# Retention and a gated feed-forward layer on one core: operand sums gated on VectorE's, loads moved five groups ahead of preparation, weight sums and evacuations moved, the last tile's products cut in pieces

## The chip, the cores and the metric

The kernel runs on one core of one Trainium2 chip. The metric is the device time of one execution in microseconds (us). A core has five engines with instruction queues of their own: TensorE (PE, with its weight loads PEld), VectorE (DVE), ScalarE (ACT), GpSimd (POOL) and SyncE (SP, which here only issues DMAs). SBUF is the working memory, PSUM the banks into which TensorE writes.

## The reference

```python
def _attn_ref(q, k, v):                      # (8, 8, 576, 64) each
    scores = scale * np.matmul(q, k.transpose(0, 1, 3, 2))
    gamma = 1.0 - 2.0 ** (-5.0 - np.arange(H))
    rel = pos[:, None] - pos[None, :]
    Dmat = np.where(rel >= 0, gamma[:, None, None] ** rel[None, :, :], 0.0)
    return np.matmul(scores * Dmat[None], v)
def _moe_ref(x, w_in, w_out):                # x: 4608 x 512, w_in: 512 x 2048, w_out: 2048 x 512
    h = x @ w_in
    return (h * np.cos(h)) @ w_out
# out = moe(attention output, the heads side by side in 512 columns)
```

Inputs and output are float32; inside, the matmul operands are bf16.

## The kernel before, in words

The 4608 tokens are 36 **groups** of 128, and ten **tiles**: one of 512 tokens (tile 0), two of 256 (tiles 1 and 2) and seven of 512 (tiles 3 to 9; `S7 = 3` is the first of these). The manual schedule keeps every engine's instructions in the order in which the Python code issues them; between engines the framework puts semaphores wherever a tile is written and read.

**Per group.** `load` issues the DMAs of fq, fk and fv (256 KB each, 128 tokens by 8 heads by 64) on SP's queue into a pool of five buffers each. `prep` runs on GpSimd: it multiplies fq and fk with the decay factors into `qks` (lines 137 and 138) and casts fv to `vb` (144). `transposes` is, from group 6 on, a DMA transpose `qks` to `qkT` on SP (153); it can't be issued before GpSimd has finished that group's `qks`. `scores` is 8 matmuls and a VectorE multiplication with the causal mask to `ret` (180, 189). `states` forms the running state in PSUM bank "b", VectorE accumulates it to `s` (260, 262) and ScalarE copies it to `sb` (253). `attn_out` puts state and scores together (280, 293), and ScalarE casts the result to `xT` (305). `unit7(g)` does this for two groups: states of g+1 and g+2, attention output of g and g+1, then scores of g+2 and g+3 (banks "a" and "b", so the second scores need bank "b" free of the states).

**Per tile.** `mm1` computes the hidden layer in eight blocks of 1024 columns: 8 matmuls, ScalarE's cosine (328), VectorE's gating multiplication to `gT` (329). In tiles 3 to 9 the second matrix product is done in the seven products of a Strassen scheme (`mm2_seven`), in the order 3, 4, 5, 2, 1, 7, 6, each 16 matmuls of 256 columns (`product`, line 430). Products 3 and 4 read `gT`; the other five read **operand sums** `gs` of quarters of `gT` (`g_sum`, 395). `sums_after` issues these in two halves, after blocks 3 and 7 of `mm1`: sum 5 on VectorE, sums 2, 1, 7 and 6 on GpSimd, each 128 x 1024. The weight sums `ws` for products 1, 6 and 7 are made once, by VectorE (373); in the kernel before between the gating multiplications of tile 2. The results are put together in four output tiles `ot` by ScalarE copies and VectorE additions (459 to 478) and stored.

**What sets the order.** Behind each store `mm2_seven` calls `feed`, which issues the preparation, transposes and loads of later groups. Each call works on the queue entries of two engines: SP gets the transpose (which waits for GpSimd) and then the next load behind it; GpSimd gets `prep`. So GpSimd's queue holds, for each of tiles 4 to 6, eight operand sums and then four preparations (tile 7 has two preparations, tiles 8 and 9 have only the sums). `at` says ahead of which product a `unit7` stands.

Of the kernel before, what the change touches and what calls it, by code (L numbers as in the profile page):

```python
# [17 lines left out]
def kernel(  # L18
# [16 lines left out]
    nc = tc.nc  # L35
# [20 lines left out]
    N_PE_T = 6  # L56

    consts = ctx.enter_context(tc.tile_pool(name="consts", bufs=1))
    first = ctx.enter_context(tc.tile_pool(name="first", bufs=1))
    ld = ctx.enter_context(tc.tile_pool(name="ld", bufs=5))  # L60
# [319 lines left out]
    def g_sum(n, x, e0, e1):  # L380
# [14 lines left out]
        (nc.vector if x == 5 or (n, x) == (S7, 1) else nc.gpsimd).tensor_tensor(  # L395
            out=tiles["gs", n, x][:, e0:e1], in0=i0, in1=i1, op=op_
        )

# [14 lines left out]

    def product(n, x):

        gT = tiles["g", n]
        if x in (3, 4, 1, 7):
            ps = psum.tile([P, 2, N2], F32, tag={3: "n", 4: "st", 1: "n", 7: "st"}[x], name="o")
            tiles["o", x] = ps
        else:  # L420
            ps = tiles["o", {5: 3, 2: 4, 6: 1}[x]]
# [6 lines left out]
        for e in range(E2):  # L428
            for j in range(2):
                nc.tensor.matmul(  # L430
                    ps[:, j],
                    lhsT=lhs[:, e, j * P : (j + 1) * P],
                    rhs=rhs[:, e, :],
                    start=(x in (3, 4, 1, 7) and e == j == 0),
                    stop=(e == E2 - 1 and j == 1),
                    skip_group_check=True,
                )

    def mm2_seven(n, at):

        s0 = starts[n] // P

# [10 lines left out]
        for x in (3, 4, 5, 2, 1, 7, 6):  # L453
            for u in at.get(x, []):
                u()
            product(n, x)
            if x == 3:
                u22 = new("a")
                nc.scalar.copy(u22, tiles["o", 3])
            elif x == 4:  # L460
                nc.vector.tensor_tensor(out=u22, in0=tiles["o", 4], in1=u22, op=ALU.add)
            elif x == 5:
                c12, u11 = new("c"), new("b")
                nc.scalar.copy(c12, tiles["o", 3])
                nc.vector.tensor_tensor(out=u11, in0=u22, in1=tiles["o", 3], op=ALU.subtract)
                store(c12, 0, 1, s0)
            elif x == 2:
                c21 = new("d")
                nc.scalar.copy(c21, tiles["o", 4])
                nc.vector.tensor_tensor(out=u22, in0=u22, in1=tiles["o", 4], op=ALU.subtract)  # L470
                store(c21, 1, 0, s0 + 1)
            elif x == 1:
                nc.vector.tensor_tensor(out=u11, in0=tiles["o", 1], in1=u11, op=ALU.add)
            elif x == 7:
                nc.vector.tensor_tensor(out=u11, in0=tiles["o", 7], in1=u11, op=ALU.add)
                store(u11, 0, 0, s0 + 2)
            elif x == 6:
                nc.vector.tensor_tensor(out=u22, in0=tiles["o", 1], in1=u22, op=ALU.add)
                store(u22, 1, 1, s0 + 3)

    loaded = prepared = transposed = 4

    def feed(s):
# [155 lines left out]
    def unit7(g, more=True):  # L639

        copy = states([g + 1, g + 2], "b")()
        attn_out([g, g + 1], "m", nc.scalar.copy)
        if more:
            scores2(g + 2)
        copy(nc.scalar.copy)

    late = []
    for n, w in enumerate(widths):
# [14 lines left out]
        for i, (et, c0, cw) in enumerate(blocks):  # L663
# [16 lines left out]
        if n == 0:  # L680
            todo = [
                (45, lambda: transposes(4, "ab")),
# [62 lines left out]
```

## Time and profile before

| | |
|---|---|
| median of 14 runs | 323.14 us (321.73 to 325.9) |
| the profiled execution | 322.88 us; span from first to last instruction 321.1 us, 1.78 us lie around it |
| mean granted TensorE clock | 0.992 |
| busy: PE / DVE / ACT / POOL | 293.2 / 209.7 / 139.3 / 218.7 us |
| PE waits for GpSimd's operand sums | 6.7 us at matmuls (7 waits), 9.0 us at weight loads (8 waits), overlapping each other |
| GpSimd's first step of a preparation waits for the fq DMA | 56.2 us, 21 waits, longest 17.4 us |

The busy times are sums over stages with different limits, so the prediction reads them tile by tile. Rows of the timeline begin with the start and the duration in us; in brackets stands the idle time of that engine just before, and what ended it. "x8" after a shape counts instructions merged in one row. SPq is SP's issuing of DMAs.

### The profile page before, as it was taken

What the parts mean: (1) busy time and instruction counts of PE and PEld (TensorE: products, weight loads), DVE (VectorE), ACT (ScalarE), POOL (GpSimd) and SP (SyncE); (2) the same over time, 40 slices, a digit from 0 to 9 for tenths busy, and PEclk for the clock granted to TensorE, in tenths of its full rate; (3) what the DMA queues carried; (4) which work ended last, traced back from release to release, by engine and by line L of the source; (5) the groups of instructions that cost most, each with busy time, mean ns of one, the idle gap of its engine ahead of it and who ended that gap; (6) DMA issues with size and microseconds to landing.
All of it is one profiled execution on the core that took longest, in us unless ns stands there. A gap on an engine that the chain in (4) does not pass through costs nothing.

```text
span 321.1 us, 6585 instructions
## 1 busy us (share of the span) xinstructions
PE 293.2 (91%) x2724; PEld 199.3 (62%) x2745; DVE 209.7 (65%) x242; ACT 139.3 (43%) x176; POOL 218.7 (68%) x179
## 2 busy tenths in 40 slices
PE   8899999996998697997999899979998899899984
PEld 3578458573587585466745674567456755784573
DVE  5767335759499962687658665776478548935852
ACT  3566225332165252643356345633464446425610
POOL 2760174445443899499957996799779946950893
PEclk9999999999799999999999999999999999999998
DMA  8999999999999994999199909990999060021012
GB/s 213 206 211 207 199 235 211 177 202 246 146 238 188 236 207 89 232 218 172 32 229 213 199 3 206 237 212 4 182 246 208 23 163 2 0 68 65 2 55 75
DMA packets 154109, 50.23 MB, mean 156 GB/s; under 512 B 140768, under 2 KB 153056, under 8 KB 154080
## 3 DMA queue, kind: packets, MB, share of 16 engines
q1 hardware_dynamic: 149856, 45.63, 74.8%
q0 software_dynamic: 4224, 4.19, 7.9%
q8 instruction: 21, 0.34, 0.5%
q14 instruction: 8, 0.07, 0.1%
HBM read 36.70 MB, written 9.44 MB: 144 GB/s over the span
## 4 chain that ended last, share of the span: by engine, by line
PE 37%; POOL 23%; DMA 18%; SPq 11%; DVE 4%; issue 3%; ACT 2%; POOLq 1%
PE h L320 21%; POOL gs L395 17%; PE o L430 11%; DMA fq<-in_q_dram 10%; SPq L112 7%; DMA fk<-in_k_dram 5%; SPq L153 3%; DMA fv<-in_v_dram 3%; POOL qks L137 3%; POOL qks L138 2%; PE o L337 2%; POOL vb L144 2%; DVE gT L329 1%; ACT cosh L328 1%; SPq L348 1%
## 5 line engine op out<-in xcount | busy, mean ns | idle before, releaser
L395 POOL TENSOR_TENSOR gs<-gT 128x1024 bf16<-128x1024 bf16 (+1 forms) x52 | 116.1, 2266 | 20.4 <-DVE gT L329 20.4
L320 PE MATMUL h<-xT,w_in_sb 128*128 128x512 bf16 (+2 forms) x820 | 127.2, 313 | 1.9 <-DVE gT L329 1.1
L329 DVE TENSOR_TENSOR gT<-h,cosh 128x1024 bf16<-128x1024 f32 x72 | 87.9, 1222 | 42.6 <-ACT cosh L328 42.6
L328 ACT ACTIVATE cosh<-h,half_pi 128x1024 f32<-128x1024 f32 x72 | 80.2, 1113 | 80.8 <-PE h L320 78.3
L320 PEld LDWEIGHTS <-w_in_sb 128*128 128x128 bf16 x832 | 75.8, 98 | 50.5 <-issue 1.9
L137 POOL TENSOR_TENSOR qks<-fq,gq 128x512 bf16<-128x512 f32 x32 | 34.9, 1090 | 58.3 <-DMA fq<-in_q_dram 56.2
L430 PEld LDWEIGHTS <-gs 128*128 128x128 bf16 x560 | 53.0, 98 | 17.1 <-POOL gs L395 9.0
L138 POOL TENSOR_TENSOR qks<-fk,gk 128x512 bf16<-128x512 f32 x35 | 37.0, 1057 | 13.5 <-DMA fk<-in_k_dram 12.8
L189 DVE TENSOR_TENSOR ret<-sc,tri 128x1024 bf16<-128x1024 f32 x32 | 37.9, 1216 | 5.0 <-PE sc L180 4.9
L430 PE MATMUL o<-ws,gs 128*128 128x256 bf16 x336 | 38.6, 273 | 2.1 <-POOL gs L395 2.1
L337 PE MATMUL o<-w_out_sb,gT 128*128 128x512 bf16 x121 | 30.4, 395 | 2.3 <-DVE gT L329 1.9
L430 PE MATMUL o<-w_out_sb,gs 128*128 128x256 bf16 x224 | 26.5, 273 | 5.4 <-POOL gs L395 4.6
L305 ACT CAST xT<-ov 128x1024 bf16<-128x1024 f32 (+1 forms) x18 | 16.5, 917 | 31.2 <-PE ov L293 31.1
L430 PE MATMUL o<-w_out_sb,gT 128*128 128x256 bf16 x224 | 25.9, 273 | 0.0
L430 PEld LDWEIGHTS <-gT 128*128 128x128 bf16 x224 | 21.7, 98 | 4.0
L144 POOL CAST vb<-fv 128x512 bf16<-128x512 f32 x32 | 20.8, 649 | 4.1 <-DMA fv<-in_v_dram 3.6
L337 PEld LDWEIGHTS <-gT 128*128 128x128 bf16 x128 | 12.1, 101 | 16.0 <-DVE gT L329 2.4
L395 DVE TENSOR_TENSOR gs<-gT 128x1024 bf16<-128x1024 bf16 (+1 forms) x15 | 17.1, 1146 | 0.4
L180 PE MATMUL sc<-qkT 64*128 64x128 bf16 x256 | 11.8, 219 | 5.7 <-DVE s L262 3.7
L253 ACT CAST sb<-s 64x256 bf16<-64x256 f32 x40 | 16.1, 403 | 0.6
L180 PEld LDWEIGHTS <-qkT 64*128 64x128 bf16 x288 | 8.6, 94 | 11.7 <-issue 8.1
L347 ACT COPY ot<-o 128x512 f32<-128x512 f32 x8 | 4.7, 588 | 21.8 <-PE o L337 21.8
(72 smaller groups left out, 181.3 us busy)
## 6 DMA issues: line engine op xcount, KB each, us to landing
out_dram<-ot SPq DMA_DIRECT2D x36, 256.0 KB, 3.5
fk<-in_k_dram SPq DMA_DIRECT2D x32, 256.0 KB, 4.9
fv<-in_v_dram SPq DMA_DIRECT2D x32, 256.0 KB, 5.0
fq<-in_q_dram SPq DMA_DIRECT2D x28, 256.0 KB, 4.0
w_in_sb<-in_moe_w_in_dram POOLq DMA_DIRECT2D x4, 512.0 KB, 8.7
w_out_sb<-in_moe_w_out_dram POOLq DMA_DIRECT2D x4, 512.0 KB, 16.1
fq<-in_q_dram SPq DMA_DIRECT2D x2, 512.0 KB, 4.5
fq<-in_q_dram SPq DMA_DIRECT2D x8, 128.0 KB, 4.5
```

The costliest lines, as they stand in the source:

```text
L112: i = nc.sync.dma_start(f[p0:p1], src[b, :, s0 : s0 + p1 - p0, :].rearrange("h s d -> s h d"))
L137: nc.gpsimd.tensor_tensor(out=qks[:, 0], in0=fq, in1=tq, op=ALU.mult)
L138: (nc.vector if g == 3 else nc.gpsimd).tensor_tensor(out=qks[:, 1], in0=fk, in1=tk, op=ALU.mult)
L144: nc.gpsimd.tensor_copy(vb, fv)
L180: nc.tensor.matmul(ps[:, he, hg, :], lhsT=qkT[d0 : d0 + D, HG + hg, :], rhs=qT[d0 : d0 + D, hg, :], start=True, stop=True,)
L189: nc.vector.tensor_tensor(out=ret.rearrange("p a b i -> p (a b) i"), in0=ps.rearrange("p a b i -> p (a b) i"), in1=mask.unsqueeze(1).to_br ...
L320: nc.tensor.matmul(ps[:, j, :], lhsT=w_in_sb[:, dg, (et + j) * P : (et + j + 1) * P], rhs=xT[:, dg, c0 : c0 + w], start=(dg == 0), stop=(d ...
L328: nc.scalar.activation(cosh, ps, ACTF.Sin, bias=half_pi, scale=1.0)
L329: nc.vector.tensor_mul(gT[:, et : et + m, c0 : c0 + w], ps, cosh)
L337: nc.tensor.matmul(ps, lhsT=gT[:, et, tsi * P : (tsi + 1) * P], rhs=w_out_sb[:, et, :], start=(et == 0), stop=(et == ET - 1),)
L395: (nc.vector if x == 5 or (n, x) == (S7, 1) else nc.gpsimd).tensor_tensor(out=tiles["gs", n, x][:, e0:e1], in0=i0, in1=i1, op=op_)
L430: nc.tensor.matmul(ps[:, j], lhsT=lhs[:, e, j * P : (j + 1) * P], rhs=rhs[:, e, :], start=(x in (3, 4, 1, 7) and e == j == 0), stop=(e == ...
```

## The change

1. **Loads.** From tile 3's first store on, `feed` prepares one group fewer at the first store of a tile and one more at the last, issues a group's transpose right behind its preparation, and only then loads, up to five groups (`LD`) ahead of the last one prepared. For groups below tile 3's first store nothing is different. GpSimd's queue has the same steps in the same order as before, up to the last tile.
2. **A gate on the sums.** The first GpSimd sum behind each VectorE sum 5 gets a dependency on it ("port free"): before, it waited only for `gT` (and for readers of the buffer).
3. **Evacuations.** VectorE's additions of a product are held in `pend` and issued ahead of the next product; where a `unit7` stands there, behind its state accumulation (`then`). In tiles 3 and 4 the units move: scores ahead of product 4 as before, `unit7(g)` from ahead of product 5 to ahead of 2, `unit7(g + 2)` from ahead of product 1 to ahead of 7.
4. **Weight sums.** The six pieces of `ws` 1, 6 and 7 move from tile 2's gating multiplications into tile 0's second matrix product.
5. **The last tile.** Sum 1 moves from GpSimd to VectorE, and products 1 and 6 are computed in three pieces one after the other (256, 128 and 128 columns, the last two in banks of their own); each piece of product 6 is added and stored by itself.

```diff
+    LD = 5
...
-        (nc.vector if x == 5 or (n, x) == (S7, 1) else nc.gpsimd).tensor_tensor(
+        i = (nc.vector if x == 5 or (x == 1 and n in (S7, len(widths) - 1)) else nc.gpsimd).tensor_tensor(
             out=tiles["gs", n, x][:, e0:e1], in0=i0, in1=i1, op=op_
         )
+        if x == 5:
+            tiles["gate"] = i
+        elif "gate" in tiles:
+            tc.add_manual_dep(
+                i.ins,
+                tiles.pop("gate").ins.name,
+                mybir.DependencyInfo(mybir.DependencyClass.Sync, mybir.DependencyReason.DATA),
+                reason="port free",
+            )
...
+        if x in (1, 6) and n == last:
+            parts = [(0, 0, N2), (1, 0, N2 // 2), (1, N2 // 2, N2)]
...
+        order = [(e, i) for e in range(E2) for i in range(len(parts))]
+        if len(parts) > 2:
+            order.sort(key=lambda u: u[1])
...
+        def add(out_, in0, in1, op_=ALU.add):
+            pend.append(lambda: nc.vector.tensor_tensor(out=out_, in0=in0, in1=in1, op=op_))
...
         for x in (3, 4, 5, 2, 1, 7, 6):
-            for u in at.get(x, []):
-                u()
-            product(n, x)
+            if x in at:
+                at[x](flush)
+            else:
+                flush()
+            parts = product(n, x)
...
+            else:
+                for (j, c0, c1), ps in zip(parts, tiles["o", 1]):
+                    add(u22[:, j, c0:c1], ps, u22[:, j, c0:c1])
+                    flush()
+                    r0 = starts[n] + 256 + j * P
+                    nc.sync.dma_start(out[r0 : r0 + P, N2 + c0 : N2 + c1], u22[:, j, c0:c1])
...
     def feed(s):
-        late_from = starts[S7] // P
+        n, r = divmod(s - starts[S7] // P, 4)
+        if n >= 0:
+            while prepared < min(NG, starts[S7] // P + 10 + 4 * n + (0, 1, 2, 4)[r]):
+                prep(prepared)
+                prepared += 1
+            while transposed < prepared:
+                transposes(transposed)
+                transposed += 1
+            while loaded < min(NG, prepared + LD):
+                load(loaded)
+                loaded += 1
+            return
         while True:
-            while prepared < min(before if s >= late_from else loaded, NG, 2 * s + 7, s + 11):
+            while prepared < min(loaded, NG, 2 * s + 7, s + 11):
...
-    def unit7(g, more=True):
+    def unit7(g, more=True, then=lambda: None):
         copy = states([g + 1, g + 2], "b")()
+        then()
         attn_out([g, g + 1], "m", nc.scalar.copy)
...
-            if n == 2 and i < 3:
-                for e in (0, 4):
-                    w_sums((1, 6, 7)[i], e, e + 4)
...
             todo = [
+                (34 + 5 * i, lambda x=x, e=e: w_sums(x, e, e + 4))
+                for i, (x, e) in enumerate((x, e) for x in (1, 6, 7) for e in (0, 4))
+            ] + [
...
-                at = {5: [lambda: unit7(g)], 1: [lambda: unit7(g + 2, n > S7)]}
+                at = {
+                    5: lambda then: unit7(g, True, then),
+                    1: lambda then: unit7(g + 2, True, then),
+                }
                 if n in (3, 4):
-                    at[4] = [lambda: scores2(g)]
+                    at = {
+                        4: lambda then: (then(), scores2(g)),
+                        2: lambda then: unit7(g, True, then),
+                        7: lambda then: unit7(g + 2, n > 3, then),
+                    }
```

SP's queue behind tile 3's first store, in the program before (the names tell the buffers apart: out is a store, fq, fk and fv are the loads of a group, qkT its transpose):

```order
L448 DMA out_0_dram<-ot_1803 128x2x256
L153 DMA_TRANSPOSE qkT_1809<-qks_1807 128x8x128
L112 DMA fq_1814<-in_q_dram 128x8x64
L112 DMA fk_1816<-in_k_dram 128x8x64
L112 DMA fv_1818<-in_v_dram 128x8x64
L448 DMA out_0_dram<-ot_1770 128x2x256
L153 DMA_TRANSPOSE qkT_1910<-qks_1908 128x8x128
```

The same place in the program of the change:

```order
L479 DMA out_0_dram<-ot_1695 128x2x256
L113 DMA fq_1699<-in_q_dram 128x8x64
L113 DMA fk_1701<-in_k_dram 128x8x64
L113 DMA fv_1703<-in_v_dram 128x8x64
L113 DMA fq_1705<-in_q_dram 128x8x64
L113 DMA fk_1707<-in_k_dram 128x8x64
L113 DMA fv_1709<-in_v_dram 128x8x64
L113 DMA fq_1711<-in_q_dram 64x8x64 x2
L113 DMA fk_1714<-in_k_dram 64x8x64 x2
L113 DMA fv_1717<-in_v_dram 64x8x64 x2
L479 DMA out_0_dram<-ot_1811 128x2x256
L154 DMA_TRANSPOSE qkT_1816<-qks_1814 128x8x128
```

The loads of three groups now stand ahead of the transpose of group 18, which waits for GpSimd; before, one group's loads stood behind it.

VectorE's queue in tile 6, from the second half of sum 5 to the last scores, before (s is the state accumulation, ot the additions of products, ret the masked scores):

```order
L395 TENSOR_TENSOR gs_3331<-gT 128x1024
L461 TENSOR_TENSOR ot<-o,ot 128x512
L262 TENSOR_TENSOR s_3448<-st,s_3151 128x256
L262 TENSOR_TENSOR s_3450<-st,s_3448 128x256
L189 TENSOR_TENSOR ret<-sc,tri 128x1024
L189 TENSOR_TENSOR ret<-sc,tri_mix 128x1024
L465 TENSOR_TENSOR ot<-ot,o 128x512
L470 TENSOR_TENSOR ot<-ot,o 128x512
L260 COPY s_3577<-st 128x256
L262 TENSOR_TENSOR s_3579<-st,s_3577 128x256
L189 TENSOR_TENSOR ret<-sc,tri 128x1024 x2
```

The same stretch in the change:

```order
L396 TENSOR_TENSOR gs_3331<-gT 128x1024
L263 TENSOR_TENSOR s_3447<-st,s_3154 128x256
L263 TENSOR_TENSOR s_3449<-st,s_3447 128x256
L472 TENSOR_TENSOR ot<-o,ot 128x512
L190 TENSOR_TENSOR ret<-sc,tri 128x1024
L190 TENSOR_TENSOR ret<-sc,tri_mix 128x1024
L472 TENSOR_TENSOR ot<-ot,o 128x512
L261 COPY s_3569<-st 128x256
L263 TENSOR_TENSOR s_3571<-st,s_3569 128x256
L472 TENSOR_TENSOR ot<-ot,o 128x512
L190 TENSOR_TENSOR ret<-sc,tri 128x1024 x2
```

Both state accumulations now stand ahead of the addition that stood before them.

VectorE's queue in the last tile, in the change (before, sum 1's pieces `gs_4086` were GpSimd's, and each of the additions was one of 128 x 512):

```order
L330 TENSOR_TENSOR gT<-h,cosh 128x1024 x4
L396 TENSOR_TENSOR gs_4082<-gT 128x1024
L396 TENSOR_TENSOR gs_4086<-gT 128x1024
L472 TENSOR_TENSOR ot<-o,ot 128x512
L472 TENSOR_TENSOR ot<-ot,o 128x512 x2
L472 TENSOR_TENSOR ot<-o,ot 128x256
L472 TENSOR_TENSOR ot<-o,ot 128x128 x2
L472 TENSOR_TENSOR ot<-o,ot 128x512
```

Sum 1's second half has moved in behind sum 5's, and the addition of product 1 is in pieces of 256, 128 and 128 columns (product 6's, behind these rows, too).

More of the change, by code (lines that the diff above doesn't have):

```diff
@@ L453, in mm2_seven @@
         for x in (3, 4, 5, 2, 1, 7, 6):
[L454 to L456 removed]
+            if x in at:
[3 more added lines that the diff above has]
+            parts = product(n, x)
             if x == 3:
                 u22 = new("a")
[L459 removed]
+                nc.scalar.copy(u22, tiles["all", 3])
             elif x == 4:
[L461 removed]
+                add(u22, tiles["all", 4], u22)
             elif x == 5:
                 c12, u11 = new("c"), new("b")
[L464 to L465 removed]
+                nc.scalar.copy(c12, tiles["all", 3])
+                add(u11, u22, tiles["all", 3], ALU.subtract)
                 store(c12, 0, 1, s0)
```

58 lines of the change are left out of this document (37 added, 21 removed).

## The prediction

> **What bounds the kernel now.** The chain of waits comes first: 37% PE is little for a kernel whose PE is busy 91% of the span, so something else decides over long stretches. The busy times, cut where `mm1` of tiles 4 to 9 begins, say where.
>
> ```profile
> PE 37%; POOL 23%; DMA 18%; SPq 11%; DVE 4%; issue 3%; ACT 2%; POOLq 1%
> core 0: us, PE busy (x) PEld busy (x) DVE busy (x) ACT busy (x) POOL busy (x), PEclk, DMA share, GB/s
> 126.27:160.17 33.90, 30.98 (x293) 20.60 (x293) 24.03 (x25) 15.00 (x19) 29.13 (x24) 1.00 0.82 157
> 160.17:192.82 32.65, 30.55 (x289) 20.33 (x288) 21.79 (x24) 15.81 (x21) 27.72 (x21) 1.00 0.82 161
> 192.82:225.47 32.65, 30.24 (x277) 20.06 (x276) 21.35 (x23) 15.00 (x19) 28.02 (x21) 1.00 0.84 162
> 225.47:258.23 32.76, 30.56 (x289) 20.37 (x289) 21.81 (x24) 15.81 (x21) 28.30 (x22) 1.00 0.82 162
> 258.23:288.95 30.72, 29.38 (x257) 19.77 (x256) 20.04 (x20) 14.24 (x17) 19.99 (x11) 1.00 0.22 61
> 288.95:321.10 32.15, 26.97 (x176) 16.71 (x175) 17.71 (x17) 10.66 (x11) 17.60 (x8) 0.97 0.15 49
> ```
>
> Each of tiles 4 to 7 has some 2 to 3 us in which PE is idle at a full clock. PE's timeline gives these gaps one by one:
>
> ```profile
> 124.52 1.92 PE L430 MATMUL o<-ws,gs 128*128 128x256 bf16 x16 [1.61 <-POOL gs L395]
> 146.72 0.31 PE L239 MATMUL st<-vb,qks 128*64 128x64 bf16 x8 [1.75 <-DVE ret L189]
> 154.58 0.40 PE L180 MATMUL sc<-qkT 64*128 64x128 bf16 x8 [0.68 <-DVE s L262]
> 183.91 1.05 PE L430 MATMUL o<-w_out_sb,gs 128*128 128x256 bf16 x8 [1.43 <-POOL gs L395]
> 187.24 0.40 PE L180 MATMUL sc<-qkT 64*128 64x128 bf16 x8 [0.57 <-DVE s L262]
> 216.56 1.05 PE L430 MATMUL o<-w_out_sb,gs 128*128 128x256 bf16 x8 [1.62 <-POOL gs L395]
> 219.89 0.40 PE L180 MATMUL sc<-qkT 64*128 64x128 bf16 x8 [0.68 <-DVE s L262]
> 249.32 1.05 PE L430 MATMUL o<-w_out_sb,gs 128*128 128x256 bf16 x8 [1.53 <-POOL gs L395]
> 252.64 0.40 PE L180 MATMUL sc<-qkT 64*128 64x128 bf16 x8 [0.56 <-DVE s L262]
> 278.75 0.40 PE L180 MATMUL sc<-qkT 64*128 64x128 bf16 x8 [1.24 <-DVE s L262]
> 316.23 1.05 PE L430 MATMUL o<-ws,gs 128*128 128x256 bf16 x8 [0.16 <-POOL gs L395]
> ```
>
> Two kinds: product 2 waits for GpSimd's operand sum, and the second scores of a unit wait for VectorE's state accumulation. GpSimd's timeline says why the sums are late:
>
> ```profile
> 108.65 2.04 POOL L137 TENSOR_TENSOR qks<-fq,gq 128x512 bf16<-128x512 f32 x1 [0.54 <-DMA fq<-in_q_dram]
> 112.21 12.25 POOL L395 TENSOR_TENSOR gs<-gT 128x1024 bf16<-128x1024 bf16 x4
> 190.08 1.03 POOL L137 TENSOR_TENSOR qks<-fq,gq 128x512 bf16<-128x512 f32 x1
> 197.35 1.04 POOL L137 TENSOR_TENSOR qks<-fq,gq 128x512 bf16<-128x512 f32 x1 [2.12 <-DMA fq<-in_q_dram]
> 202.47 1.46 POOL L137 TENSOR_TENSOR qks<-fq,gq 128x512 bf16<-128x512 f32 x1 [2.21 <-DMA fq<-in_q_dram]
> 205.59 17.16 POOL L395 TENSOR_TENSOR gs<-gT 128x1024 bf16<-128x1024 bf16 x8
> 267.85 17.59 POOL L395 TENSOR_TENSOR gs<-gT 128x1024 bf16<-128x1024 bf16 x8 [7.23 <-DVE gT L329]
> 298.57 17.60 POOL L395 TENSOR_TENSOR gs<-gT 128x1024 bf16<-128x1024 bf16 x8 [13.13 <-DVE gT L329]
> ```
>
> From 190.08 GpSimd prepares two groups without a pause (5.15 us, to 197.35 - 2.12), waits twice for fq loads, and begins tile 6's sums at 205.59, with nothing idle before them: preparation made them late. Where no preparation precedes (267.85), they wait for `gT`, and product 2 waits for nothing. The loads are late because SP issues one group's at a time, behind a transpose that itself waits for GpSimd:
>
> ```profile
> 118.67 0.97 SPq L448 DMA_DIRECT2D out_dram<-ot  x1
> 126.49 1.23 SPq L153 DMA_TRANSPOSE qkT<-qks  x1
> 127.77 0.57 SPq L112 DMA_DIRECT2D fq<-in_q_dram  x1
> ```
>
> Behind the store of 118.67 SP stands still for nearly 7 us, and only then issues the next load.
>
> **The loads and the gate: product 2's waits.** With three groups' loads ahead of that transpose, each preparation finds data issued a tile earlier. GpSimd's cycle is then 17.16 us of sums, 4 x 2.58 = 10.3 us of preparations, 0.6 for the extra v cast of some tiles: 28.1. The sums' start is set by the gate, sum 5's first half:
>
> ```profile
> 202.33 0.69 DVE L395 TENSOR_TENSOR gs<-gT 128x1024 bf16<-128x1024 bf16 x1
> 209.24 1.11 DVE L395 TENSOR_TENSOR gs<-gT 128x1024 bf16<-128x1024 bf16 x1
> 274.65 2.57 DVE L395 TENSOR_TENSOR gs<-gT 128x1024 bf16<-128x1024 bf16 x1
> 305.37 2.58 DVE L395 TENSOR_TENSOR gs<-gT 128x1024 bf16<-128x1024 bf16 x1
> ```
>
> It stands 9.51 us behind the start of tile 6; with its 0.69 us and 0.15 for the hand-over (an estimate, from the 0.16 us that PE waits for GpSimd in the row of 316.23) the sums begin at T + 10.35 instead of T + 12.8. With 0.5 us lost to VectorE they end at T + 28.0, four preparations at T + 38.4 to 39.0; the next gate opens at T + 30.35 + 10.35 = 40.7 (30.35 is tile 6's 32.65 less its two waits). So the gate is reached some 2 us early, and PE becomes the bound. Behind the gated sum stand GpSimd's other sums and the preparations, for which SP's transposes wait: all of them still come sooner than before. The fifth sum (product 2's second half) is done at T + 21.6; PE, without its wait, wants it at 216.56 - 1.62, T + 22.1. So 1.43, 1.62 and 1.53 go in tiles 5 to 7; if that half microsecond of cover is gone, the wait comes back by as much as is missing. The second store of tile 3 now stands behind twelve more DMA issues; it only frees a buffer that is wanted two tiles later.
>
> What the gate can cost lies between two kinds of rows. A GpSimd sum running from 205.59 ends every 2.145 us; the VectorE sum of 209.24 ended at 210.35, just after such an end (209.88): it waits out one GpSimd instruction. In the rows of 274.65 and 305.37 it came 0.07 us ahead of such an end, lost the next turn too and took 2.57. With the gate, the third end falls at +0.83 + 3 x 2.145 = 7.27 us behind the first half's start, the second half comes at +6.91: 0.36 ahead. The known winner came 0.64 ahead, the known loser 0.07. I take a win (0.8 us, hidden by products 3 and 4) and keep the loss for a rival.
>
> The Trainium skill (SBUF — State Buffer, "Who interferes with whom") says that a VectorE instruction with two SBUF inputs and a GpSimd instruction that reads SBUF exclude each other for the whole instruction, whoever starts first. The rows above agree (0.69 us alone, 2.57 blocked); by this rule every second half of sum 5 is exposed, and with a turn lost in each of tiles 4 to 8 the sum would come out as in the second case below, 314.7.
>
> **The evacuations: the scores' waits.**
>
> ```profile
> 218.26 0.69 DVE L470 TENSOR_TENSOR ot<-ot,o 128x512 f32<-128x512 f32 x1 [2.86 <-ACT ot L469]
> 219.32 0.42 DVE L262 TENSOR_TENSOR s<-st,s 128x256 f32<-128x256 f32 x1
> ```
>
> VectorE adds product 2 only when ScalarE's copy is done, and the states stand behind it, the scores behind them. In the new order the states (0.87 us) run while PE does `attn_out` and the first scores (1.4 us): 0.57, 0.68, 0.56 of tiles 5 to 7, 0.68 of tile 4 and 1.24 of tile 8 go. The delayed additions hold nothing up: the next writer of their banks comes a product later. In tile 4 product 5 now stands between the scores and the states, 1.8 us of cover for `ret`: 1.75 goes too. Tile 8's is between 0.6 (a turn lost) and 1.24.
>
> **The beginning and tile 3: nothing.** Below tile 3's first store SP's and GpSimd's queues are as they were. Group 17's fq lands just before 108.65, the sums follow from 112.21 to 124.46, and PE waits for the last (124.52). What PE gains earlier by weight sums moved out of tile 2 and by the better order of tile 3 ends in a longer wait here. Weight sums hold up GpSimd wherever they stand:
>
> ```profile
> 73.99 2.72 DVE L373 TENSOR_TENSOR ws<-w_out_sb 128x1024 bf16<-128x1024 bf16 x2
> ```
>
> Two took 2.72 us instead of 1.4, by collision; in tile 0, where GpSimd prepares too, I expect as many collisions. Net 0; bounds: -1 us (the 2.04 of 108.65 back at 1.04) and +1.
>
> **The last tile.**
>
> ```profile
> 210.47 0.62 PE L280 MATMUL ov<-qkT,sb 128*128 128x128 bf16 x8
> 217.91 0.40 PE L280 MATMUL ov<-qkT,sb 128*128 128x128 bf16 x4
> 317.31 0.69 DVE L478 TENSOR_TENSOR ot<-o,ot 128x512 f32<-128x512 f32 x1 [1.39 <-PE o L430]
> ```
>
> GpSimd's eight sums end at 316.17 and release product 6's last matmuls (316.23 to 317.28). Without sum 1 they are six: three from about 299.65 (behind VectorE's pair) to 306.1; VectorE's second pair to 307.2; three more to 313.65. PE, following, ends product 6 at 315.8: 1.5 us earlier. Four more matmuls of 128 columns cost 0.22 us, 0.055 each, half of one of 256 (16 in 1.92, 8 in 1.05: 0.109), so cutting costs nothing; if the weight loads set the pace (19.77 us for 256 in tile 8's window, 0.077 each) it costs 32 x 0.022 = 0.7. The last addition is 128 columns: some 0.28 instead of 0.69, by the 0.42 of a 256-column row; the store's 3.1 us behind it I leave, though it is a quarter of the bytes. Together -1.9; bounds -2.6 (a store faster by a quarter of its 3.1 us) and -0.5 (0.7 for weights, 0.7 for a turn lost to GpSimd).
>
> **The sum.** Tile 4: 1.75 + 0.68 = 2.43; tile 5: 2.00; tile 6: 2.30; tile 7: 2.09; tile 8: 1.24; tile 9: 1.9. Together 11.96. The profiled execution (span 321.1) took 322.88 us, 0.26 below the median, so 310.9 for it and 311.1 for the median.
>
> **The rivals.** *A turn lost at the port in every tile.* Sum 5's second half ends 1.8 us later; the scores wait 0.6 in tiles 5 to 8, and tile 4, where `ret` follows it directly, 1.2: 3.6 us, 314.7. For it: two of the rows above; against: 0.36 us of lead. *Loads are hidden no better.* If SP's new order brings data no earlier (DMAs are busy 82% in these tiles, and three groups in a row queue up), GpSimd keeps its 5 us of waits, the 4.58 of product 2's waits stay, and half of tile 4's ret wait: 316.5. Against: five groups of buffers are 30 us of lead. *Slower: transposes too late.* Two of a tile's four now stand together behind the last store and behind all stores and loads of SP's queue. Group 25's is issued about T + 10, its scores come at T + 24: it decides from 14 us of delay on, and to end slower than 323.1 five tiles must each wait 2.4 us more beyond that; with 3 us each, 326. SP's stall above is 7 us, half the slack. *Change without effect on the end*: if only tiles 8 and 9 gain, 320.
>
> **Chances.** My forecast 0.62, the port 0.17, the loads 0.10, late transposes 0.05, only the last tiles 0.04, within 0.3% (1 us, about what a measurement of this kernel tells from no change) 0.02. The range takes the forecast's bounds below (311.1 - 1 - 0.7 = 309.4, rounded down) and the two next cases above. Faster 0.93, same 0.02, slower 0.05.
>
> **What would show it.** Right: in tiles 5 to 7 a period near 30.5 us, no PE wait for `gs` ahead of product 2, none for `s` ahead of scores, GpSimd's sums begin behind idle time released by VectorE's sum, no fq waits past 130 us; tile 4 starts at 126 as before; the end comes 32.15 - 1.9 us behind tile 9's start. Wrong: tile 4 starting elsewhere, sum 5's second half at 2.57 us, or preparations still waiting for DMAs.

## The result and the profile after

The changed kernel took 308.26 us (median of 10 runs, 307.24 to 309.78) against 322.9 us for the kernel before (48 runs): the ratio is 0.9544, with a 95% interval of 0.9517 to 0.957. That is 14.6 us, where 12.0 were forecast; the forecast's time was 311.1 us, and its range ended at 309. The profiled execution of the change took 307.11 us, 15.8 less than that of before (322.88). The two profiles differ by 1.1 us more than the medians do; where single executions scatter is said further below. A few executions of some kernels took several us longer than the rest of the same kernel: the medians of the experiments leave these out, and two profiles are of such executions (before's feed in the change, 324.65 us; three sums behind `ret`, 309.2 us), so that only waits, and the clock behind them, are read from them.

The chain of waits of the changed kernel, shares of the span by engine; it was 37% PE and 23% POOL:

```profile
span 305.4 us, 6636 instructions
PE 81%; DVE 5%; POOL 4%; issue 2%; SPq 2%; DMA 2%; ACT 1%; POOLq 1%; DVEq 0%
```

The busy times of the changed kernel, cut where `mm1` of tiles 4 to 9 begins (length of the stretch, then each engine's busy time with its instructions, granted clock, DMA share, GB/s):

```profile
core 0: us, PE busy (x) PEld busy (x) DVE busy (x) ACT busy (x) POOL busy (x), PEclk, DMA share, GB/s
124.19:155.43 31.24, 30.75 (x293) 20.54 (x293) 23.15 (x25) 15.00 (x19) 29.13 (x24) 1.00 1.12 218
155.43:185.66 30.23, 30.12 (x288) 20.36 (x288) 21.32 (x24) 15.81 (x21) 27.21 (x21) 1.00 0.96 178
185.66:215.67 30.01, 29.91 (x276) 20.14 (x276) 20.95 (x23) 15.00 (x19) 27.14 (x20) 1.00 0.91 176
215.67:245.91 30.24, 30.14 (x289) 20.39 (x289) 21.31 (x24) 15.80 (x21) 28.32 (x23) 1.00 0.42 97
245.91:275.22 29.31, 29.20 (x257) 19.73 (x257) 18.41 (x20) 14.19 (x17) 19.56 (x11) 1.00 0.21 55
275.22:305.40 30.18, 26.31 (x192) 17.34 (x191) 17.69 (x23) 10.66 (x11) 13.26 (x6) 1.00 0.16 53
```

Set beside the same table of before:

| tile | 4 | 5 | 6 | 7 | 8 | 9 |
|---|---|---|---|---|---|---|
| period before, us | 33.90 | 32.65 | 32.65 | 32.76 | 30.72 | 32.15 |
| period after | 31.24 | 30.23 | 30.01 | 30.24 | 29.31 | 30.18 |
| shorter by | 2.66 | 2.42 | 2.64 | 2.52 | 1.41 | 1.97 |
| forecast | 2.43 | 2.00 | 2.30 | 2.09 | 1.24 | 1.9 |
| PE's idle time (period less busy), before | 2.92 | 2.10 | 2.41 | 2.20 | 1.34 | |
| after | 0.49 | 0.11 | 0.10 | 0.10 | 0.11 | |
| idle time gone | 2.43 | 1.99 | 2.31 | 2.10 | 1.23 | |
| PE busy less by | 0.23 | 0.43 | 0.33 | 0.42 | 0.18 | |

The idle time that went is the forecast to 0.01 us in each of tiles 4 to 8. What the forecast lacks stands in the last row, 1.59 us together. Tile 4 began 2.08 us earlier in this pair of executions, where nothing was forecast.

PE's timeline of the changed kernel in tile 6 has no idle time in brackets left. These are its rows from product 3 on and, last, the scores of the second unit:

```profile
199.80 3.33 PE L452 MATMUL o<-w_out_sb,gT 128*128 128x256 bf16 x29
203.06 0.32 PE L240 MATMUL st<-vb,qks 128*64 128x64 bf16 x8
204.43 0.62 PE L181 MATMUL sc<-qkT 64*128 64x128 bf16 x16
204.98 3.67 PE L452 MATMUL o<-w_out_sb,gs 128*128 128x256 bf16 x32
209.85 0.64 PE L181 MATMUL sc<-qkT 64*128 64x128 bf16 x16
```

Products 5 and 2 run as one row of 32 (204.98), where product 2 waited 1.62 us at 216.56 before. The scores of a unit's two groups run as one row of 16 (204.43 and 209.85), where the second unit's second scores waited 0.68 us at 219.89 before. The sums, on GpSimd's timeline, then on VectorE's, and one more row of GpSimd's:

```profile
110.16 12.22 POOL L396 TENSOR_TENSOR gs<-gT 128x1024 bf16<-128x1024 bf16 x4
165.78 17.17 POOL L396 TENSOR_TENSOR gs<-gT 128x1024 bf16<-128x1024 bf16 x8 [3.02 <-DVE gs L396]
196.04 17.18 POOL L396 TENSOR_TENSOR gs<-gT 128x1024 bf16<-128x1024 bf16 x8 [2.87 <-DVE gs L396]
226.02 17.17 POOL L396 TENSOR_TENSOR gs<-gT 128x1024 bf16<-128x1024 bf16 x8 [1.78 <-DVE gs L396]
195.17 0.69 DVE L396 TENSOR_TENSOR gs<-gT 128x1024 bf16<-128x1024 bf16 x1
202.08 0.81 DVE L396 TENSOR_TENSOR gs<-gT 128x1024 bf16<-128x1024 bf16 x1
202.30 2.58 POOL L396 TENSOR_TENSOR gs<-gT 128x1024 bf16<-128x1024 bf16 x1
```

GpSimd now reaches the gate 1.8 to 3.0 us early and waits for VectorE's first half; in tile 6 its sums begin at T + 10.38 (196.04 less 185.66; forecast T + 10.35). VectorE's second half (202.08) takes 0.81 us; the last row is GpSimd's fourth sum by itself, which began 0.22 us after it and took 2.58 us instead of some 2.12: here GpSimd is the one that waits.

### The profile page after: what moved, and what is told of

Same layout as the page of the kernel before. It is cut to its first block, busy times and chain, and to the rows that moved or that the text cites. A ratio compares the mean times of both kernels' runs of the same rounds, so it can differ in the third digit from the quotient of the medians.

```text
span 305.4 us, 6636 instructions
## 1 busy us (share of the span) xinstructions
PE 292.0 (96%) x2740; PEld 200.9 (66%) x2761; DVE 203.1 (66%) x248; ACT 139.2 (46%) x176; POOL 211.6 (69%) x177
## 4 chain that ended last, share of the span: by engine, by line
PE 81%; DVE 5%; POOL 4%; issue 2%; SPq 2%; DMA 2%; ACT 1%; POOLq 1%; DVEq 0%
PE h L321 35%; PE o L452 26%; PE o L338 9%; PE ov L294 3%; PE sc L181 3%; POOL gs L396 3%; DVE gT L330 3%; PE ov L281 3%; DMA fk<-in_k_dram 2%; SPq L113 2%; ACT cosh L329 1%; PE st L240 1%; DVE w_out_sb L374 1%; POOLq L803 1%; POOL qks L139 1%
## 5 line engine op out<-in xcount | busy, mean ns | idle before, releaser
L396 POOL TENSOR_TENSOR gs<-gT 128x1024 bf16<-128x1024 bf16 (+1 forms) x50 | 111.3, 2263 | 30.4 <-DVE gs L396 30.4
L452 PEld LDWEIGHTS <-gs 128*128 128x128 bf16 x576 | 55.2, 100 | 14.3 <-POOL gs L396 6.1
L452 PE MATMUL o<-ws,gs 128*128 128x256 bf16 (+1 forms) x352 | 39.5, 272 | 0.0
L452 PE MATMUL o<-w_out_sb,gs 128*128 128x256 bf16 x224 | 28.0, 283 | 4.9 <-POOL gs L396 4.8
L472 DVE TENSOR_TENSOR ot<-o,ot 128x512 f32<-128x512 f32 (+2 forms) x32 | 19.6, 618 | 14.7 <-PE o L452 14.6
L338 PE MATMUL o<-w_out_sb,gT 128*128 128x512 bf16 x121 | 28.8, 380 | 0.4 <-issue 0.2
L145 POOL CAST vb<-fv 128x512 bf16<-128x512 f32 x32 | 19.5, 610 | 3.9 <-DMA fv<-in_v_dram 3.6
L472 DVE TENSOR_TENSOR ot<-ot,o 128x512 f32<-128x512 f32 x14 | 9.6, 684 | 12.6 <-ACT ot L502 9.5
L396 DVE TENSOR_TENSOR gs<-gT 128x1024 bf16<-128x1024 bf16 (+1 forms) x17 | 12.9, 774 | 0.4
```

The source lines that it names most:

```text
L145: nc.gpsimd.tensor_copy(vb, fv)
L338: nc.tensor.matmul(ps, lhsT=gT[:, et, tsi * P : (tsi + 1) * P], rhs=w_out_sb[:, et, :], start=(et == 0), stop=(et == ET - 1),)
L396: i = (nc.vector if x == 5 or (x == 1 and n in (S7, len(widths) - 1)) else nc.gpsimd).tensor_tensor(out=tiles["gs", n, x][:, e0:e1], in0=i ...
L452: nc.tensor.matmul(dst[i], lhsT=lhs[:, e, j * P : (j + 1) * P], rhs=rhs[:, e, c0:c1], start=(x in (3, 4, 1, 7) and e == 0 and (i == 0 or l ...
L472: pend.append(lambda: nc.vector.tensor_tensor(out=out_, in0=in0, in1=in1, op=op_))
```

## The experiments

Two questions were open. Which parts carry the gain: *theory A* says that early loads and the gate need each other, since sums that start sooner meet VectorE at the port they share, and that evacuations, weight sums and the last tile add to that separately; its rival, that loads alone carry it and the gate is an ornament. And where the 2.6 us more than forecast come from: the part ahead of tile 4, or waits that cost more than their rows show. Each experiment is timed against the kernel before.

**Loads alone** (the kernel before with the new `feed`; its core is shown):

```diff
+            while prepared < min(NG, starts[S7] // P + 10 + 4 * n + (0, 1, 2, 4)[r]):
...
+            while loaded < min(NG, prepared + LD):
```

> The kernel before with only the new order of loads, transposes and preparations (no gate, old evacuations, old last tile). Theory: the waits of product 2 for GpSimd's sums go in tiles 5 to 7. If a wait costs what its row shows, that is 4.6 us; if it costs 0.17 more (the end of the last matmul, which runs on while the next one could already start), 5.1 us. But without the gate the sums start together with VectorE's sum 5, and its second half should take 2.6 us as in tiles 8 and 9 before, so the scores' waits of about 0.6 us in tiles 5 to 7 grow to 1.2: about 1.9 us back. Together 3 us below before, about 320. Rival: the port does not matter, 317.8 to 318.3.

Measured: 323.12 us (10 runs), ratio 1.0015 [0.9976, 1.0054]: nothing gained. Its timelines of GpSimd, VectorE and PE in tile 6, and two of its windows:

```profile
203.66 17.62 POOL L396 TENSOR_TENSOR gs<-gT 128x1024 bf16<-128x1024 bf16 x8 [4.55 <-DVE gT L330]
210.37 2.11 POOL L396 TENSOR_TENSOR gs<-gT 128x1024 bf16<-128x1024 bf16 x1
210.45 2.58 DVE L396 TENSOR_TENSOR gs<-gT 128x1024 bf16<-128x1024 bf16 x1
214.01 0.40 PE L181 MATMUL sc<-qkT 64*128 64x128 bf16 x8 [0.82 <-DVE s L263]
146.68 0.32 PE L240 MATMUL st<-vb,qks 128*64 128x64 bf16 x8 [2.72 <-DVE ret L190]
125.27:161.63 36.36, 32.57 (x294) 21.62 (x292) 25.00 (x25) 15.01 (x19) 35.01 (x30) 0.95 1.24 219
194.03:225.88 31.85, 30.35 (x279) 20.20 (x277) 22.64 (x23) 15.12 (x19) 27.30 (x20) 1.00 0.85 164
```

The loads do their work: GpSimd idles 4.55 us ahead of its sums, and product 2 waits for nothing. The second row is one of the eight sums by itself: it began 0.08 us ahead of VectorE's second half, took its usual 2.11 us, and VectorE waited it out. So the second half of sum 5 takes 2.57 or 2.58 us in each of tiles 4 to 9, and the scores wait for the states behind it (0.82 here, 1.25 and 1.24 in tiles 5 and 7). Tile 6 is still 0.80 us shorter than before (31.85 against 32.65), yet tile 4, where `ret` stands behind that sum and PE waits 2.72 us for it, is 2.46 us longer (36.36 against 33.90; what became of the clock there stands in the last section).

**The gate alone** (the kernel before with the dependency):

```diff
+        if x == 5:
+            tiles["gate"] = i
+        elif "gate" in tiles:
+            tc.add_manual_dep(
...
```

> The kernel before with only the gate on GpSimd's first sum. Theory (gate and loads need each other): in tiles 4 to 7 the sums begin late, behind the preparations, so the gate waits for nothing and nothing changes there; in tiles 8 and 9, where the sums wait for gT, VectorE's sum 5 wins its turn (0.8 us instead of 2.57): tile 8 loses its scores' wait of 1.24 us (with what follows 1.4), tile 9 its 0.71 at product 5 but not the end, which the eight sums set. Time 1.4 us below before, 321.2. Rival (the gate is worth 7 us by itself, as the change without it was 7.3 slower): 315.5.

Measured: 321.58 us (12), 0.9966 [0.9944, 0.9987]. PE's and VectorE's timelines in tile 6 and VectorE's in tile 8:

```profile
216.73 1.05 PE L439 MATMUL o<-w_out_sb,gs 128*128 128x256 bf16 x8 [1.66 <-POOL gs L395]
209.38 1.14 DVE L395 TENSOR_TENSOR gs<-gT 128x1024 bf16<-128x1024 bf16 x1
274.76 0.81 DVE L395 TENSOR_TENSOR gs<-gT 128x1024 bf16<-128x1024 bf16 x1
```

In tiles 5 to 7 the late sums never reach the gate ahead of VectorE, and product 2 waits as before; in tiles 8 and 9, where nothing is prepared, the second half falls from 2.57 to 0.81 us. Tile 8's wait for `s` is gone with it and the tile is 1.33 us shorter (29.39 against 30.72), which is about the 1.2 us gained; tile 9 is not shorter. Tile 4 is 0.65 us shorter in this profile too, against the expectation (its second half took 0.96 us instead of 1.61, and PE waited 1.10 us for `ret` instead of 1.75); whether the gate did that is open, as tile 4 also began at another time (127.10).

**Both** (the two diffs above together):

> The kernel before with the new order of loads and the gate, all else as before. Theory: the loads alone gave nothing because sum 5 lost its turn in every tile; with the gate it wins, so product 2's waits go (1.43, 1.62, 1.53, each 0.17 more: 5.1 us) and tile 8's 1.4; the scores' waits of the second unit stay, and tile 4's wait for ret shrinks from 1.75 to about 1 us. Together 7 to 7.5 us below before: 315.3. Rival (additive parts: loads 0, gate 1.4): 321.3.

Measured: 315.18 us (4), 0.9771 [0.9749, 0.9792]: some 7.5 us, where the one alone gave nothing and the other 1.2. VectorE's sum and PE's scores in tile 6:

```profile
206.22 0.81 DVE L396 TENSOR_TENSOR gs<-gT 128x1024 bf16<-128x1024 bf16 x1
215.07 0.40 PE L181 MATMUL sc<-qkT 64*128 64x128 bf16 x8 [0.68 <-DVE s L263]
```

The waits of product 2 are gone, those for `s` are those of the kernel before: they belong to the evacuations. Tiles 5 to 7 are 1.59, 1.80 and 1.71 us shorter than before, where the rows of the waits that went said 1.43, 1.62 and 1.53: each wait was worth 0.16 to 0.18 us more than its row.

**The change without the gate:**

```diff
-        if x == 5:
-            tiles["gate"] = i
-        elif "gate" in tiles:
-            tc.add_manual_dep(
...
```

> The change without the dependency of GpSimd's first sum on VectorE's sum 5. Theory (the gate sets which engine wins the port at sum 5's second half): without it the sums begin about as soon, but their third end falls 0.07 us behind VectorE's request as in tiles 8 and 9 before; the second half takes 2.6 us in tiles 4 to 8, the scores wait 0.6 us there and 1.2 in tile 4: about 3.6 us slower than the change, 311.9. Rival (the gate is idle, the turns are won anyway): within 0.5 us of 308.3.

Measured: 315.55 us (6), 0.9784 [0.9743, 0.9825], 7.3 us more than the change and twice the 3.6 expected. VectorE's timeline in tiles 6 and 9 and PE's in tile 9:

```profile
206.90 2.58 DVE L396 TENSOR_TENSOR gs<-gT 128x1024 bf16<-128x1024 bf16 x1
291.58 3.23 DVE L396 TENSOR_TENSOR gs<-gT 128x1024 bf16<-128x1024 bf16 x2
296.00 1.89 PE L321 MATMUL h<-xT,w_in_sb 128*128 128x512 bf16 x8 [1.68 <-DVE gT L330]
304.19 1.91 PE L443 MATMUL o<-w_out_sb,gs 128*128 128x256 bf16 x16 [1.07 <-DVE ot L463]
```

The turn at the port is lost again in every tile. Tiles 4 to 8 are 1.03, 0.82, 0.40, 0.81 and 0.82 us longer than in the change (3.88; the prediction's rival put these at 3.6), and the last tile 2.85 (33.03 against 30.18): there VectorE computes two pairs of sums, 3.23 and 3.21 us instead of 1.29 and 1.70, and PE waits both times. The rival falls: the gate is no ornament.

**The change with before's feed** (the new branch of `feed` taken out):

> The change with the loads, transposes and preparations in the old order. Theory: GpSimd's preparations wait for fq again, the sums begin 2 us late, and product 2 waits 1.4 to 1.6 us in tiles 5 to 7, each worth 0.17 more: 5.1 us, perhaps 1 more in tile 4: 313.4 to 314.4. Rival (the gate and the evacuations carried the gain): under 310.

Measured: 317.35 us (5), 0.9835 [0.9808, 0.9861], 9.1 us more than the change and 3 us more than expected. Beside the gate alone (321.58) it is 4.2 us faster, of which the last tile (1.9, below) and the weight sums (1.2 to 1.9, below) can account for most; for the evacuations 1 us or less is left. With late loads they seem to bring little gain either. In its profile PE waits for GpSimd's sums ahead of product 2 again, 0.84, 2.14, 0.62 and 2.14 us in tiles 4 to 7 (before: none in tile 4, then 1.43, 1.62 and 1.53). So what PE gained elsewhere may come back as a longer wait there, but that one profile can't size it.

**The old evacuations** (the change, with each addition issued at once):

```diff
-            pend.append(lambda: nc.vector.tensor_tensor(out=out_, in0=in0, in1=in1, op=op_))
+            nc.vector.tensor_tensor(out=out_, in0=in0, in1=in1, op=op_)
```

> The change with each addition issued at once behind its product, as before, instead of behind the state accumulation (units where the change has them). Theory: the second scores of the second unit wait for the state accumulation again, 0.57, 0.68 and 0.56 us in tiles 5 to 7 and about 0.7 in tile 4. By the rows alone the time grows by 2.5 us (310.8); with 0.17 us more for each wait, by 3.2 (311.5). A tile's period should grow by the idle time of its row plus 0.17: that tests the size of the term that the prediction had too small. Rival (the additions' place is hidden now): 308.3.

Measured: 310.71 us (5), 0.9626 [0.9601, 0.9651], 2.45 us more. PE's timeline and the window of tile 6:

```profile
213.78 0.40 PE L181 MATMUL sc<-qkT 64*128 64x128 bf16 x8 [0.68 <-DVE s L263]
188.51:219.36 30.85, 30.17 (x278) 20.14 (x276) 21.06 (x23) 15.00 (x19) 27.17 (x21) 1.00 0.86 170
```

The waits for `s` are back with before's sizes (0.57, 0.68 and 0.57 in tiles 5 to 7), while the periods grew by 0.82, 0.84 and 0.81: again 0.16 to 0.25 us more than each row. These three make 2.47 us. Tile 4 shows no such wait, where some 0.7 us was expected, and is 0.43 us longer (31.67).

**The old last tile** (the change, with sum 1 on GpSimd and products 1 and 6 whole):

```diff
-x == 1 and n in (S7, len(widths) - 1)
+x == 1 and n == S7
...
-    last = len(widths) - 1
+    last = len(widths)
```

> The change with the last tile as before (sum 1 on GpSimd, products 1 and 6 whole, one store). Theory: the last tile takes 32.1 us instead of 30.2, so 1.9 us more, 310.2. Rival (with the gate the last tile's sums come soon enough): 308.3.

Measured: 310.19 us (6), 0.962 [0.9591, 0.9648], 1.9 us more than the change, as forecast for this step; in the profile the last tile takes 32.53 us, 2.35 more.

**The weight sums** were tried both ways, the change with them back in tile 2, and the kernel before with them in tile 0:

```diff
-                (34 + 5 * i, lambda x=x, e=e: w_sums(x, e, e + 4))
-                for i, (x, e) in enumerate((x, e) for x in (1, 6, 7) for e in (0, 4))
...
+            if n == 2 and i < 3:
+                for e in (0, 4):
+                    w_sums((1, 6, 7)[i], e, e + 4)
```

> The change with one part undone: the six weight-sum pieces stand again between tile 2's gating multiplications. Question: tile 4 began at 124.19 us instead of 126.27, and the prediction had 0 there. Theory A (in tile 2 the weight sums took the shared port from GpSimd's preparations, and these set the chain of transposes and loads; in tile 0 they don't): tile 3's GpSimd sums begin at about 112.2 again, tile 4 at 126.2, and the time is 2 us above the change, about 310.3. Rival B (the head differs by chance from one execution to the next, from the landing times of DMAs): the median stays within 0.5 us of the change, about 308.3, and the sums begin anywhere from 110 to 112. Rival C (TensorE's earlier tile 3 shortens the chain): then tile 4 begins late only by as much as TensorE's products of tile 3 are late, about 3 us, 311.

> The kernel before with only the weight sums moved to tile 0. Theory A: tile 3's GpSimd sums begin near 110.2, tile 4 near 124.2, time 2 us below before (about 320.9). Rival B: no difference in the median (322.9, within 0.5). TensorE's waits in tile 2 (1.89 and 1.18 us for gT) go in either case and, if tile 3 is bound by GpSimd's sums, come back as a longer wait there.

Measured: back in tile 2, 310.11 us (5), 0.9599 [0.9546, 0.9652], 1.9 us more than the change, though the two intervals overlap; alone in tile 0, 321.57 us (12), 0.9954 [0.9924, 0.9984], 1.2 to 1.5 us less than before. Together they say that the place is worth some 1 to 2 us, which the prediction put at nothing; neither figure is good to much better than 1 us. The profiles fit only in part. Back in tile 2, tile 4 began at 126.95, as expected; alone in tile 0 it began at 126.58, where 124.2 was expected, but that was the longest execution of the twelve (323.0 us).

**Tile 3's sums.** In the change PE waits longest at 112.33, for GpSimd's sum 2 (row in the last section). Three versions take sums from GpSimd there. The first gives sum 2 to VectorE:

```diff
-(x == 1 and n in (S7, len(widths) - 1))
+(x == 1 and n in (S7, len(widths) - 1)) or (x == 2 and n == S7)
```

> The change with sum 2 of tile 3 also on VectorE (two pieces of 128 x 1024; GpSimd keeps 7 and 6). Theory: tile 3 is bound by GpSimd, whose sums come behind group 17's preparation; TensorE waits 4.6 us for sum 2 there. With two GpSimd sums fewer (4.2 us) the last one ends near 118.3, product 6 near 120.2, and everything behind is about 4 us earlier: 304.3. Rival: tile 3's end is set by the groups' preparations and loads as well, so that tile 4's sums are late by what tile 3 gains: 306 to 308.

Measured: 305.27 us (6), 0.9461 [0.9411, 0.9511], 3 us less than the change. VectorE's and PE's timelines:

```profile
105.29 4.48 DVE L396 TENSOR_TENSOR gs<-gT 128x1024 bf16<-128x1024 bf16 x3
112.19 0.42 PE L240 MATMUL st<-v_odd,qks 128*64 128x64 bf16 x8 [2.76 <-POOL qks L139]
```

Three sums on VectorE took 4.48 us instead of some 2.5 (in the change, 1.82 for two of them, one twice as wide, and 0.69 for a half), beside GpSimd's preparations; `ret` stands behind them, ends at 112.04, and PE waits 2.76 us. The row names a `qks` of GpSimd, but these states read groups prepared long before; that PE waited for `ret`, 0.15 us ahead of its start, is the likelier reading. The second version therefore puts sum 2's second half and sum 1 behind `ret`, with sum 7 first on GpSimd:

```diff
-                for x, e in ((5, 4), (2, 4), (1, 0), (7, 0), (6, 0)):
+                for x, e in ((5, 4), (7, 0), (6, 0)):
...
+                            [g_sum(n, x, e, E2) for x, e in ((2, 4), (1, 0)) if n == S7],
```

> The change with tile 3's sums 2 and 1 on VectorE, sum 2's second half and sum 1 behind the masking of the first scores (ret) instead of ahead of it. Where sum 2 merely moved to VectorE, three sums ahead of ret took 4.48 us instead of 2 (blocked turns against GpSimd's preparations), TensorE waited 2.76 us for ret and then ran some 2 us at half its clock. Theory: ret comes 3 us sooner, TensorE no longer waits there, and tile 3's end is set by GpSimd's sums 7 and 6 (8.1 us from about 110 to 113): 1 to 2 us faster than 305.3, so 303.3 to 304.3. Rival (the chain of preparations, whose start varies by 3 us from execution to execution, sets it): 305.3.

Measured: 305.59 us (5), 0.9461 [0.9438, 0.9485]: no better, as its rival had it. PE's timeline in tiles 3 and 4:

```profile
111.15 0.40 PE L181 MATMUL sc<-qkT 64*128 64x128 bf16 x8 [1.21 <-DVE s L263]
121.19 1.92 PE L452 MATMUL o<-ws,gs 128*128 128x256 bf16 x16 [2.09 <-POOL gs L396]
150.72 0.40 PE L181 MATMUL sc<-qkT 64*128 64x128 bf16 x8 [0.55 <-DMA qkT<-qks]
```

One wait became several: the scores now wait for states behind VectorE's sums, product 6 for GpSimd. And tile 4, begun 1.2 us earlier than in the change (122.95), meets transposes that are not there yet, and tile 5 begins at 155.40, as in the change (155.43). The third version moves sum 7 to VectorE too, behind `ret`:

```diff
-                for x, e in ((5, 4), (2, 4), (1, 0), (7, 0), (6, 0)):
+                for x, e in ((5, 4), (6, 0)):
...
+                            [g_sum(n, x, e, E2) for x, e in ((2, 4), (1, 0), (7, 0)) if n == S7],
```

> As the run before, with sum 7 of tile 3 on VectorE as well, so that GpSimd keeps one sum (4.05 us). Theory: no GpSimd sum sets tile 3's end; products run through: 1 to 2 us faster still, 302 to 303. Rival: VectorE's three sums (0.7 + 1.3 + 1.3 us, more when GpSimd holds the port) stand ahead of the state accumulation, the second scores of the first unit wait 1 to 3 us, and GpSimd's gain is lost: 304 to 305.5.

Measured: 304.38 us (4), 0.9438 [0.9417, 0.9459], the fastest kernel of the study, 3.9 us below the change, but short of the 302 to 303 expected and inside the rival's 304 to 305.5. The rival's wait is there in the profile: the scores wait 3.22 us for `s` behind VectorE's sums. Against the first two versions the intervals overlap, so which of the three is best stays open.

## Why the prediction was right or wrong

Working through the profiled pair, 15.77 us less against 11.96 forecast: 2.08 ahead of tile 4, 1.59 of PE's busy time in tiles 4 to 8, 0.07 in tile 9 and 0.07 outside the span make up the 3.8 that are missing.

1. **The loads and the gate: right.** Product 2's waits went in tiles 5 to 7, GpSimd came early, and the sums began where they were put. The second half of sum 5 took 0.78 to 0.81 us in all of tiles 4 to 8, as taken. Only the picture behind it was off: the known loser (274.65) was not a VectorE sum that came ahead of a turn and lost it. GpSimd's rows overlap by some 0.04 us, and its next sum had begun at 274.54; the loser came 0.11 us behind that start.
2. **The port rival's mechanism was right without the gate, and its price too small:** 3.6 us counted tiles 4 to 8, which cost 3.88, and the last tile costs 2.85 more when its two pairs of VectorE sums are blocked. The rule of the Trainium skill (SBUF — State Buffer, "Who interferes with whom") under which every second half is exposed gives the lock to whichever begins first, and agrees with both kinds of rows: 0.08 us behind, VectorE waits 1.9 us (loads alone), 0.22 us ahead, GpSimd waits 0.46 (the change). The rule was no argument against the gate, which decides who begins first.
3. **The evacuations: right in place for tiles 5 to 7** (no wait for `s` remains), 2.45 us by the experiment. Tile 8's 1.24 us stood in this term but belongs to the gate: with the gate alone the wait went, and with the old evacuations it did not come back. Of tile 4's 1.75 us for `ret`, loads and gate took some (0.94 is left in both together).
4. **Failed: the size of a wait.** Each wait was counted with the idle time of its row. In the profile, which models the ends of matmuls, one runs on while the next already starts, as these rows of PE in the changed kernel's tile 4 show, where the first ends at 142.88, by its start and duration:

```profile
140.96 1.92 PE L452 MATMUL o<-w_out_sb,gT 128*128 128x256 bf16 x16
142.72 1.91 PE L452 MATMUL o<-w_out_sb,gs 128*128 128x256 bf16 x16
```

   The overlap is 0.16 us. Ahead of a wait that end lies beside nothing and is counted as busy; without the wait it disappears below the next matmul. So a wait costs its row and some 0.17 us: two waits went in each of tiles 5 to 7 (0.33 to 0.43 more than forecast), one in tile 8 (0.18); tile 4 shows less (0.23 for two). Loads with the gate (0.16 to 0.18 a wait) and the old evacuations (0.16 to 0.25) show it one wait at a time. The term is 1.59 us.
5. **Failed: "Net 0" for the beginning and tile 3.** By the medians some 1.0 us lies there (14.6 less the 13.6 of tiles 4 to 9), with the ratio's interval worth 0.9 us to either side. It stood at the edge of the bounds given, and tile 4 did start elsewhere, which was named as a sign of being wrong. The weight sums' two experiments give 1 to 2 us. The premise "in tile 0 I expect as many collisions" held for GpSimd. These are its lengthened preparation rows, three in tile 2 of the kernel before and three in tile 0 of the changed one; undisturbed, they take 1.04 us (qks) and 0.61 (vb):

```profile
71.43 0.96 POOL L144 CAST vb<-fv 128x512 bf16<-128x512 f32 x1
74.92 1.24 POOL L138 TENSOR_TENSOR qks<-fk,gk 128x512 bf16<-128x512 f32 x1 [0.20 <-DMA fk<-in_k_dram]
76.11 1.07 POOL L144 CAST vb<-fv 128x512 bf16<-128x512 f32 x1
38.51 1.49 POOL L138 TENSOR_TENSOR qks<-fq,gq 128x512 bf16<-128x512 f32 x1 [17.46 <-DMA fq<-in_q_dram]
46.37 1.33 POOL L138 TENSOR_TENSOR qks<-fq,gq 128x512 bf16<-128x512 f32 x1 [1.25 <-DMA fq<-in_q_dram]
47.66 1.51 POOL L139 TENSOR_TENSOR qks<-fk,gk 128x512 bf16<-128x512 f32 x1
```

   GpSimd lost 1.0 us in tile 2 before and 1.2 us in tile 0 after, and by the same count 0.7 to 1.1 and 0.9 to 1.5 us in the profiles of the experiments. So fewer collisions with its preparations do not explain the gain: what failed is the step from as many collisions to the same end. In the change PE's two waits for `gT` in tile 2 (1.89 and 1.18 us) went with the weight sums; how a gain there reaches tile 4 stays open, and with the weight sums alone in tile 0 PE waited 2.20 us for a transpose instead (at 83.67). What was said of PE held in this trace: it ended in a longer wait for GpSimd, 4.62 us at 112.33, where before PE waited 2.09 us for `ret` and 1.61 for GpSimd. One profile can't size it: GpSimd's sums of tile 3 began at 110.16 in the change, at 111.22, 111.74 and 113.10 with the old tail, the old evacuations and without the gate, which are the same code or nearly so up to there. From tile 5 on there is no such scatter: from its start to the span's end the change takes 149.97 us, the version with weight sums in tile 2 150.01, that with sum 2 on VectorE 150.00.
6. **The last tile: right in sum, 1.97 against 1.9,** with two terms off that cancel. PE's last matmul ends 26.47 us behind the tile's start (301.69) instead of 28.33, so 1.86 earlier where 1.5 were forecast, and what follows it takes 3.71 us instead of 3.82, where 0.4 were forecast.

```profile
296.25 5.44 PE L452 MATMUL o<-ws,gs 128*128 128x256 bf16 x64
301.73 0.49 DVE L472 TENSOR_TENSOR ot<-o,ot 128x128 f32<-128x128 f32 x2 [0.47 <-PE o L452]
```

   In this pair of rows (PE's and VectorE's last in the changed kernel) the additions are short as expected; the stores behind them are not shorter for being smaller: from the last addition's end to the end of the span it is 3.18 us, before 3.10.

## What to carry to other kernels

When data comes sooner, ask which two engines will now meet: here earlier loads were worth nothing until a dependency decided who takes the shared port first, and that dependency was worth little without them. Price a removed wait of PE with its row and the tail of the matmul ahead of it, some 0.17 us here for each wait. Compare executions stage by stage, and leave to the medians every stage whose start differs between executions of equal code.

## What the hardware showed that was not expected

**TensorE's clock halved behind long waits.** PE's row in tile 3 of the change, and windows behind it (change), behind the 2.72 us of the loads alone, and behind the 1.75 us of the kernel before; the granted clock is the third number from the right:

```profile
112.33 1.89 PE L452 MATMUL o<-w_out_sb,gs 128*128 128x256 bf16 x8 [4.62 <-POOL gs L396]
112.30:114.40 2.10, 1.89 (x8) 1.04 (x9) 0.00 (x0) 0.00 (x0) 2.10 (x2) 0.50 1.28 240
114.40:119.00 4.60, 4.60 (x24) 3.25 (x24) 0.69 (x1) 0.59 (x1) 4.60 (x2) 0.57 1.29 254
146.60:150.00 3.40, 3.32 (x50) 2.69 (x51) 1.50 (x3) 1.19 (x2) 3.40 (x2) 0.58 1.11 250
146.72:150.00 3.28, 3.28 (x61) 2.81 (x62) 2.25 (x4) 1.71 (x3) 3.28 (x2) 1.00 1.33 227
```

Eight matmuls took 1.89 us where the kernel before shows 1.05, so a long wait costs its length and then again in what follows it; waits of 1.75 and 2.09 us left the clock at 1.00. Length alone does not decide it: in the one profile of before's feed in the change, a wait of 2.14 us ahead of 189.45 was followed by a clock of 0.59 (from 191 to 194), another of 2.14 us ahead of 255.26 by one of 1.00 (from 257 to 260). The Trainium skill (TensorE: Matmul & The Clock Gate, "What's actually happening") says that the clock is half after at least one idle window of about 3.4 us, of a window that runs freely; halving behind 2.72 us of idle time lies under that figure, and no run here shows from which length on it sets in.

**A tenth of a microsecond decided 1.8 us.** VectorE's second half came 0.08 us behind the start of a GpSimd sum in the loads alone (210.45 against 210.37) and took 2.58 us; 0.22 us ahead of one in the change (202.08 against 202.30) it took 0.81, and GpSimd's took 2.58. The gate starts GpSimd's sums 0.87 us behind VectorE's first half (196.04 against 195.17) instead of some 0.1, and 7.3 us of the whole hung on it.
